# Attention and a mixture of experts on one core: the attention planned anew with other transfer times

## The chip, the core and the metric

The kernel runs on one core of a Trainium2 chip. The core has five engines with instruction queues of their own, each worked off in order: TensorE (PE in the rows; its weight loads stand apart as PEld), VectorE (DVE), ScalarE (ACT), GpSimd (POOL) and SyncE (SP), which here only issues transfers. An engine waits for another by semaphores. The metric is the device time of one execution in microseconds (us).

## What is computed

The first half is a linear attention with a complex decay, for 4 batches, 8 heads, 768 steps and a head size of 48; the second half gives its 3072 rows of 384 to 8 experts of 384 rows each and runs two matrix products per expert.

```python
mag = np.sqrt(a_re * a_re + a_im * a_im)
scale = np.minimum(mag, 0.999) / (mag + 1e-06)
a_re_n, a_im_n = (a_re * scale, a_im * scale)
...
for t in range(S):
    ar, ai = (a_re_n[:, :, t, :, None], a_im_n[:, :, t, :, None])
    new_re = ar * S_re - ai * S_im
    new_im = ar * S_im + ai * S_re
    kv = np.einsum('bhd,bhe->bhde', k[:, :, t], v[:, :, t])
    S_re, S_im = (new_re + kv, new_im)
    y[:, :, t] = np.einsum('bhd,bhde->bhe', q[:, :, t], S_re)
...
order = np.argsort(-flat)          # greedy: best score first, each expert takes N // E rows
...
h = np.maximum(x[mask] @ w1[e], 0.0)
out[mask] = h @ w2[e]
```

## The kernel before

**Tiling.** The attention is cut into 8 groups (`GROUPS`, two per batch) of three units of 128 steps: 24 units. Group 0 is worked on in two pieces (one unit, then two), group 7 too (two, then one). A group is first prepared elementwise, on tiles of 128 x 1152 (or 384 and 768 for the pieces), on ScalarE and VectorE. Each unit then has its own steps on TensorE.

**The steps and the names in the rows.** A step's short name is the key that the planner gives it; in the rows an instruction shows by the tiles that it writes and reads.

- Loads, issued by SyncE (group 0's `ai` by ScalarE): `la` is `ar<-in_a_re`, `li` is `ai<-in_a_im`, `lk` is `kq<-in_kq`, `lv` is `V<-in_v`. Of `ar` and of `ai` there is one buffer, so that the next group's load waits until the readers of this one (`F1`, `F3`, `F4` for `ar`; `F2`, `F3` for `ai`) are done.
- ScalarE, per group: `F1` (`s<-ar,cb`, a square), `F2` (`s<-ai`), `F5` (`zi<-s,cb`), `F7` (`s<-s,cb`), `F8` (`s<-zi`), `F10` (`s<-s,cb`), `G1` (`s<-zi`), `G2` (`zi<-zi`), `A1` and `A2` (`p<-p`), `T2` (`p<-neg`), and the cosine and sine, `T3` (`CS<-p,cb`) and `T1` (`CS<-neg`). Between the two sets of functions a table is loaded (ACT_TABLE_LOAD).
- VectorE, per group: `F4` (`neg<-ar`), `F3` (`p<-ar,ai`), `F6` (`s<-s,s`, the sum of `F1` and `F2`), `F9` (`zi<-s`), `F11` (`p<-p,s`), `S` (scans `zi<-zi,s`), `N0` (scans into `neg`), `N2` (`neg<-neg`), `G3` (`kq<-kq,s`) and `G5` (`kq<-kq,zi`).
- Per unit: `RQ` on VectorE multiplies by cosine and sine (`f<-kq,CS`, needs `T1` and `T3`); `K` is six transfers issued by SyncE that stack it (`KQ<-f`); on TensorE `SC` (`sc<-KQ`, scores, two halves), `FL` (`kp<-ident,KQ`), `ST` and `CA` (`U<-V,kt` and `U<-W,ident`, the carried state), `MX` (`y<-...`, the unit's output) and `FN` (`xp<-pick,xT`). VectorE masks the scores (`MK`, `am<-sc,mask`, two halves; `MX` waits for both), scales the state (`WM`, `W<-U,KQ`) and reduces the router's scores (`LR`, `lg<-xp`; after unit 17 with a maximum and a copy). ScalarE empties PSUM (`KC`, `XC`, `XE`). `BE` is five small VectorE steps on the first 18 units' scores for the router.
- `FI` are matmuls without use (`sc<-mask,f`) that keep TensorE busy ahead of a unit's scores; the table `FILL` has their number, in three portions per unit. A unit's `FI` waits for its own `RQ` and for the mask of the unit before.

**What sets the order.** The steps are put into a list with costs, wishes (`prio`, about the unit's number) and dependencies. `in_order` (line 179) then plays the engines against each other with a model of the costs: on each engine the ready step with the lowest wish plus offset (`OFF`, line 679, one number per kind of step) goes next. The order that comes out is the program's order on each engine, SyncE's transfers too; an engine never overtakes. A transfer's time in this model is made of `FLIGHT` and `ARRIVE`, and of its data time (`moved`, line 311, `K_DATA`). The model's times decide nothing else: on the chip only the order, the dependencies and `FILL` are left of it. The expert half is planned apart.

Of the kernel before, what the change touches and what calls it, by code (L numbers as in the profile page):

```python
# [21 lines left out]
B, H, S, D = 4, 8, 768, 48  # L22
N, DM, E, FF = B * S, H * D, 8, 1024
CAP = N // E
NT = N // 128
GC = 3
T = GC * 128
# [229 lines left out]
def attention(nc, real, tc, z, kq_in, a_re, a_im, v_tok, xd, later):  # L257
# [12 lines left out]
    for i in range(2):  # L270
        x = con.tile([128, GC * 384 + 16], F32, name=f"V{i}")
# [9 lines left out]
    act = nc.scalar.activation  # L281

    ops = []
    made = {}

    def op(key, eng, cost, prio, fn, deps=()):
        kind = key[0][0] if type(key[0]) is tuple else key[0]
        o = Op(eng, cost, fn, [made.get(d) for d in deps], prio)
        o.kind = kind + ("<" if prio < EARLY else ">" if prio >= LATE else "")
        ops.append(o)  # L290
        made[key] = o
        if o.kind.rstrip("<>") in ("lk", "lv"):
            moved(o, 128, (24 if key[0] == "lk" else 12) * T)
        return o

    def dve(n):
# [8 lines left out]
    def sca(n, bias=False):  # L305
        return n / 1200 + (0.19 if bias else 0.094)
# [1 line left out]
    def pool(n):  # L308
        return n / 460 + 0.08

    def moved(x, rows, nbytes):
        x.data = LOADS * rows * (9 + nbytes / 26) / 16e3

    G = len(GROUPS)
    cuts = [CUTS.get(gi, [(0, GC)]) for gi in range(G)]
# [3 lines left out]
    def get(name, gi, shape=None, p=ew, **kw):  # L319
        if (name, gi) not in tiles:  # L320
            tiles[name, gi] = p.tile(shape or [128, 3, T], F32, name=name, **kw)
        return tiles[name, gi]
# [8 lines left out]
    def last_of(stage, gi):  # L331
        return [(stage, gi, j) for j in range(len(cuts[gi]))] if gi >= 0 else []

    def free(name, stages, gi):
        return [x for s in stages for x in last_of(s, gi - BUFS[name])]
# [4 lines left out]
    def load_a(gi, j, name, src):  # L340
        b, c0, n = GROUPS[gi]
        lo, hi = cuts[gi][j]
        w = slice(lo * 384, hi * 384)
        q = nc.scalar if gi == 0 and name == "ai" else nc.sync
        return lambda: q.dma_start(
            get(name, gi, [128, 3 * T], p=ld, bufs=1)[:, w], src[b, c0 // GC, :, w])
# [17 lines left out]
    def elementwise(gi, j, at):  # L364
        b, c0, _ = GROUPS[gi]
        lo, hi = cuts[gi][j]
        n = hi - lo
# [4 lines left out]
        def G_(name, **kw):  # L372
            return get(name, gi, **kw)[..., cols]
# [4 lines left out]
        def I_(name):  # L378
            return get(name, gi)[:, lo * 384:hi * 384].rearrange("p (i t) -> p i t", i=3)

        def add(stage, eng, cost, fn, deps):
            op((stage, gi, j), eng, cost, at, fn, deps)
# [2 lines left out]
            return [(s_, gi, j) for s_ in ss]  # L385

        first = -60.0 + 30.0 * j if gi == 0 else at
        op(("li", gi, j), "dma" if gi else "act", 0.6, first - (0 if gi else 2000.0), load_a(gi, j, "ai", a_im), free("ai", ["F2", "F3"], gi))
        op(("la", gi, j), "dma", 0.6, first, load_a(gi, j, "ar", a_re), free("ar", ["F1", "F3", "F4"], gi))
        for x in ops[-2:]:  # L390
            moved(x, 128 * (1 if n == GC else 3), 12 * T if n == GC else 512 * n)
        add("F1", "act", sca(N3, True), lambda: act(G_("s1", bufs=S1_BUFS), I_("ar"), AF.Square, bias=z.cb[:, 0:1]),
            k_("la") + free("s1", ["F11", "F6"], gi))
        add("F2", *(("dve", dve(N3), lambda: v.tensor_tensor(
# [61 lines left out]
    def turns(i):  # L456
# [10 lines left out]

        f_free = [("K", i - F_BUFS), ("FI", i - F_BUFS, len(FILL.get(i - F_BUFS, ())) - 1)] if i >= F_BUFS else []
        op(("P0", i), "pool", 0.75, i, lambda: g.tensor_copy(
# [19 lines left out]
    def unit(i):  # L489
        gi, c = i // GC, i % GC  # L490
# [10 lines left out]
        def keep(n):  # L501
            if ("sc", 0) not in mine:
                mine["sc", 0] = ps.tile([128, 4, 128], F32, name="sc", bufs=2)
            for _ in range(n):
                nc.tensor.matmul(mine["sc", 0].rearrange("p h t -> p (h t)"), tiles["f", i][:, 0, 0, 128:256].bitcast(BF)[:, 1::2],
                                 z.mask.bitcast(BF)[:, None].to_broadcast([128, 2, 256]), start=True, stop=True)
        parts = FILL.get(i, ())
        for n, x in enumerate(parts):
# [100 lines left out]
        op(("FN", i), "pe", 0.9, at + 0.6, turn, [("XC", i), ("XE", i - 2), ("LR", i - 2)])  # L609
        op(("XE", i), "act", 0.371, at, out, [("FN", i), ("XS", i - 2)])  # L610
        op(("XS", i), *(("pool", 1.1) if i < NT - 2 else ("act", 0.33)), at, store, [("XE", i)])
        moved(ops[-1], 128, 4 * DM)
        op(("LR", i), "dve", 0.105 if i % 6 < 5 else 0.4, at, logits, [("FN", i)])

    def load(key, cost, at, fn, deps=()):
# [2 lines left out]
    for gi in range(G):  # L618
        for j in range(len(cuts[gi])):
            elementwise_at = gi * GC + cuts[gi][j][0]  # L620
            if j == 0:
                load(("lk", gi), 0.6, elementwise_at + 0.5, load_kq(gi), turned(gi - KQ_BUFS))
                if gi < 2:
                    load(("lv", gi), 0.6, elementwise_at + 0.6, load_v(gi))
            elementwise(gi, j, elementwise_at)
            if gi == 1:
                for x in (("lv", 0), ("lk", 1), ("lv", 1)):
                    made[x].deps.append(made["la", 1, 0])
        for c in range(GC):
            turns(gi * GC + c)  # L630
            unit(gi * GC + c)
        if gi + 2 < G:
            load(("lv", gi + 2), 0.6, elementwise_at + 4, load_v(gi + 2),
                 [("MX", gi * GC + c) for c in range(GC)] + [("ST", gi * GC + c) for c in range(GC)])
# [8 lines left out]
    for o in ops:  # L643
        o.prio += OFF.get(o.kind, 0.0)
    for o in in_order(ops, STEP, HOP, DMA_WAIT, DMA_DONE, START, SLACK):
# [25 lines left out]
BY_DMA = []  # L671
SLACK = 0.0
DMA_WAIT = 0.1
FLIGHT, ARRIVE = 1.3, 0.7
K_DATA, LOADS = 3.3, 1.15
DMA_DONE = 1.1
LATER = [2.4, 4.6, 0.9, 3.6]
START = dict(pe=0.0, act=0.3, dve=2.6, pool=4.3, dma=0.65)
OFF = {"A1": 10.399, "A2": -9.822, "BE": 0.131, "CA": -2.118, "F1": -1.107, "F10": 3.443, "F11": 7.184, "F2": -0.925, "F3": 5.421, "F4": 5.223, "F5": -4.22, "F6": 3.011, "F7": -5.852, "F8": -2.715, "F9": -5.359, "FI": 6.816, "FI<": 9.377, "FL": 9.859, "FL<": -5.873, "FN": 12.915, "G1": 1.011, "G2": -1.21, "G3": -11.062, "G4": -0.449, "G5": -6.433, "K": -5.895, "KC": -14.0, "LR": -0.075, "MK": -7.142, "MX": 7.176, "N0": 3.163, "N2": 4.716, "P0": 12.184, "RQ": 2.776, "S": 7.92, "SC": 10.153, "SC<": -1.898, "ST": 11.563, "ST<": -6.332, "T1": 8.558, "T2": 10.974, "T3": -7.584, "TL": -6.667, "WM": -3.298, "XC": -9.548, "XC<": -8.705, "XE": 10.454, "XS": 9.28, "la": -9.643, "la<": -6.574, "later": 0.869, "li": -8.149, "li<": -7.975, "lk": -3.51, "lv": -2.528, "table": -8.414}
CHAIN = ("scalar", "vector", "tensor", "gpsimd", "sync")  # L680
F_BUFS, KC_BUFS = 4, 5
FILL = {0: (6, 6, 6), 1: (2, 2, 2), 2: (4, 4, 4), 3: (2, 2, 2), 5: (6, 6, 6), 7: (4, 4, 4), 8: (1, 1, 1), 9: (3, 3, 3), 10: (1, 1, 1), 11: (3, 3, 3), 12: (3, 3, 3), 13: (2, 2, 2)}
SQ = ()
EARLY, LATE = 0, 99

# [830 lines left out]
```

## Time and profile before

| | |
|---|---|
| time, median of 3 runs | 488.61 us (488.24 to 489.17) |
| the profiled execution | 488.22 us; its span, first to last instruction, 486.4 us |
| busy in the span: PE, PEld | 430.7 us (89%), 386.3 us (79%) |
| busy in the span: DVE, ACT, POOL | 400.9 us (82%), 307.9 us (63%), 124.5 us (26%) |
| the chain that ended last | PE 69%, issue 12%, ACT 7%, DVE 6%, DMA 3% |

The attention takes the first 223 us or so of the span, the router and the experts the rest. Busy time is the time in which an engine had an instruction running; PEld lies beside PE. Matmuls are pipelined and the ends of their rows are modelled, so that the start of the next row is the better measure of how long one took. A row's idle time, in brackets, stands before the row, with what ended it.

### The profile page before, as it was taken

To read this page: it belongs to the slowest core of one execution; us is meant where nothing else is said; L and a number is where in the kernel's file an instruction comes from. 1 tells how busy PE (TensorE), PEld (TensorE's weight loads), DVE (VectorE), ACT (ScalarE), POOL (GpSimd) and SP (SyncE) were. 2 spreads that over 40 slices of the span, in tenths; PEclk is the share of its full clock that TensorE was granted. 3 is DMA by queue.
4 is the path that set the end of the run, shared out by engine and by line. 5 is a ranking of instruction groups with operands and counts; after the bars stand their busy time and mean duration, and the time that the engine had idled before them with its cause. 6 is when DMAs were issued, how large, how long until landed. Compare 5 with 4: busy or idle time off the path is not lost.

```text
span 486.4 us, 9831 instructions
## 1 busy us (share of the span) xinstructions
PE 430.7 (89%) x3632; PEld 386.3 (79%) x3632; DVE 400.9 (82%) x1023; ACT 307.9 (63%) x582; POOL 124.5 (26%) x218
## 2 busy tenths in 40 slices
PE   0019999999999999996389999999999999999996
PEld 0006887889789899985279799999999999999995
DVE  6999999999999999945869989898898999434250
ACT  7999988999889849712055538375472837442341
POOL 7321020304021411223131223140413335040202
PEclk9999999999999999998589999999999999999999
DMA  7807876868796846521162616280724438420001
GB/s 254 330 2 202 277 252 204 280 212 279 219 290 206 275 145 176 164 82 65 37 214 85 285 50 219 123 313 15 282 75 165 194 112 345 161 98 0 34 16 50
DMA packets 33104, 82.52 MB, mean 170 GB/s; under 512 B 4352, under 2 KB 23552, under 8 KB 29984
## 3 DMA queue, kind: packets, MB, share of 16 engines
q1 hardware_dynamic: 25632, 41.96, 27.6%
q0 software_dynamic: 6848, 38.95, 21.6%
q10 hardware_dynamic: 576, 0.98, 0.5%
q8 instruction: 29, 0.48, 0.4%
q14 instruction: 19, 0.16, 0.1%
HBM read 53.49 MB, written 9.44 MB: 129 GB/s over the span
## 4 chain that ended last, share of the span: by engine, by line
PE 69%; issue 12%; ACT 7%; DVE 6%; DMA 3%; POOL 1%; POOLq 1%; SPq 0%; ACTq 0%; DVEq 0%
PE acc L136 30%; PE sc L136 12%; PE y L136 8%; PE U L136 8%; PE xp L136 4%; PE kp L136 3%; ACT s L136 3%; PE cnt L136 3%; ACT p L136 1%; ACT L278 1%; DMA ai<-in_a_im 1%; DVE ind L136 1%; POOL out L136 1%; DVE neg L136 1%; DMA KQ<-f 1%
## 5 line engine op out<-in xcount | busy, mean ns | idle before, releaser
L136 PE MATMUL acc<-w2h,hh 128*128 128x384 f32 x192 | 62.5, 345 | 0.2 <-DVE hl L136 0.2
L136 PE MATMUL acc<-w2h,hl 128*128 128x384 f32 x192 | 62.1, 344 | 0.0
L136 PE MATMUL acc<-w2l,hh 128*128 128x384 f32 x192 | 61.9, 344 | 0.1
L136 PE MATMUL acc<-xl,w1h 128*128 128x384 f32 x192 | 61.2, 343 | 0.1
L136 PE MATMUL acc<-xh,w1l 128*128 128x384 f32 x192 | 61.2, 343 | 0.0
L136 PE MATMUL acc<-xh,w1h 128*128 128x384 f32 x192 | 60.0, 339 | 0.0
L136 PE MATMUL sc<-mask,f 128*128 128x512 bf16 x111 | 28.2, 400 | 35.1 <-DVE f L136 35.1
L136 ACT ACTIVATE hh<-acc 128x384 fp32r<-128x384 f32 x64 | 30.7, 491 | 38.6 <-PE acc L136 38.1
L136 POOL DMA_INDIRECT out<-ot,idx x24 | 25.5, 1063 | 105.5 <-ACT ot L136 100.4
L136 DVE SCALAR_TENSOR_TENSOR hl<-acc,hh 128x384 fp32r<-128x384 f32 x64 | 34.7, 550 | 21.6 <-ACT hh L136 21.1
L136 PEld LDWEIGHTS <-f 128*128 128x128 bf16 x111 | 10.5, 102 | 48.1 <-DVE f L136 35.1
L136 PE MATMUL sc<-KQ 96*128 96x128 f32 x384 | 48.1, 277 | 0.0
L136 PEld LDWEIGHTS sc<-KQ 96*128 96x128 f32 x384 | 45.1, 192 | 0.8 <-issue 0.7
L136 ACT ACTIVATE parts<-cnt 32x8 f32<-32x8 f32 x120 | 20.1, 168 | 39.4 <-PE cnt L136 37.2
L136 DVE TENSOR_TENSOR f<-kq,CS 128x1536 f32<-128x1536 f32 x24 | 41.6, 1749 | 1.1 <-ACT CS L136 0.7
L136 DVE TENSOR_TENSOR am<-sc,mask 128x512 f32<-128x512 f32 x48 | 31.9, 680 | 6.6 <-PE sc L136 6.2
L136 POOL DMA_DIRECT2D xd<-x x22 | 13.3, 607 | 90.6 <-ACT x L136 90.6
L136 PE MATMUL y<-am,V 128*64 128x128 f32 x384 | 36.5, 278 | 0.0
L136 PEld LDWEIGHTS acc<-w2h,hh 128*128 128x128 f32 x192 | 35.6, 189 | 0.6 <-DVE hl L136 0.6
L136 DVE TENSOR_TENSOR ind<-m,thr 128x768 bf16<-128x768 f32 (+1 forms) x45 | 33.8, 768 | 2.6 <-PE thr L136 2.3
L136 PEld LDWEIGHTS acc<-w2l,hh 128*128 128x128 f32 x192 | 35.6, 188 | 0.3 <-DVE w2l L136 0.2
L136 PEld LDWEIGHTS acc<-w2h,hl 128*128 128x128 f32 x192 | 35.7, 188 | 0.0
(203 smaller groups left out, 1109.2 us busy)
## 6 DMA issues: line engine op xcount, KB each, us to landing
KQ<-f SPq DMA_DIRECT2D x144, 128.5 KB, 2.7
kq<-in_kq SPq DMA_DIRECT2D x8, 1152.0 KB, 7.4
V<-in_v SPq DMA_DIRECT2D x8, 576.0 KB, 5.4
xd<-x POOLq DMA_DIRECT2D x22, 192.0 KB, 3.1
ar<-in_a_re SPq DMA_DIRECT2D x6, 576.0 KB, 4.5
ai<-in_a_im SPq DMA_DIRECT2D x6, 576.0 KB, 5.4
ar<-in_a_re SPq DMA_DIRECT2D x2, 384.0 KB, 5.0
ar<-in_a_re SPq DMA_DIRECT2D x2, 192.0 KB, 4.6
```

Source lines behind the costliest of these rows:

```text
L136: r = f(*a, **k)
L278: real.scalar.add_instruction(ins)
```

## The change

The planner's numbers are changed, and with them the order of the attention's steps. A transfer's data time is now a number for each kind of load, no longer worked out from its bytes; the other numbers of the transfer model, all offsets and the table of fillers are new. The steps, their tiles, buffers and dependencies stay; the fillers are 108 in place of 111, spread over the units in another way.

```diff
         if o.kind.rstrip("<>") in ("lk", "lv"):
-            moved(o, 128, (24 if key[0] == "lk" else 12) * T)
+            moved(o, RATE_Q if key[0] == "lk" else RATE_V)
...
-    def moved(x, rows, nbytes):
-        x.data = LOADS * rows * (9 + nbytes / 26) / 16e3
+    def moved(x, us):
+        x.data = us
...
-        op(("li", gi, j), "dma" if gi else "act", 0.6, first - (0 if gi else 2000.0), load_a(gi, j, "ai", a_im), free("ai", ["F2", "F3"], gi))
-        op(("la", gi, j), "dma", 0.6, first, load_a(gi, j, "ar", a_re), free("ar", ["F1", "F3", "F4"], gi))
+        op(("li", gi, j), "dma" if gi else "act", 0.43, first - (0 if gi else 2000.0), load_a(gi, j, "ai", a_im), free("ai", ["F2", "F3"], gi))
+        op(("la", gi, j), "dma", 0.43, first, load_a(gi, j, "ar", a_re), free("ar", ["F1", "F3", "F4"], gi))
         for x in ops[-2:]:
-            moved(x, 128 * (1 if n == GC else 3), 12 * T if n == GC else 512 * n)
+            moved(x, RATE_A * n / GC)
+        if not (gi or j):
+            ops[-1].data += WAKE
...
-        moved(ops[-1], 128, 4 * DM)
+        moved(ops[-1], RATE_X)
...
-FLIGHT, ARRIVE = 1.3, 0.7
-K_DATA, LOADS = 3.3, 1.15
+FLIGHT, ARRIVE = 1.38, 0.4
+K_DATA, RATE_A, RATE_Q, RATE_V, RATE_X, WAKE = 4.0, 1.3, 3.8, 1.5, 0.46, 1.0
...
-FILL = {0: (6, 6, 6), 1: (2, 2, 2), 2: (4, 4, 4), 3: (2, 2, 2), 5: (6, 6, 6), 7: (4, 4, 4), 8: (1, 1, 1), 9: (3, 3, 3), 10: (1, 1, 1), 11: (3, 3, 3), 12: (3, 3, 3), 13: (2, 2, 2)}
+FILL = {0: (6, 6, 6), 1: (4, 4, 4), 2: (2, 2, 2), 3: (3, 3, 3), 5: (1, 1, 1), 6: (6, 6, 6), 7: (2, 2, 2), 8: (3, 3, 3), 9: (1, 1, 1), 10: (4, 4, 4), 11: (1, 1, 1), 12: (1, 1, 1), 13: (1, 1, 1), 16: (1, 1, 1)}
```

`OFF`, the table of offsets, has a new number for each of its 56 kinds of step; what it does shows in the order alone. The first place is ScalarE's queue before the first cosine and sine (tiles `CS`). The tiles of 3x128 and 3x256 are group 0's two pieces; 1152 wide are groups 1 and 2. Before:

```order
L136 ACTIVATE zi<-zi 128x3x256
L136 ACTIVATE s_310<-ar,cb 128x1152
L136 ACTIVATE s_270<-s_270,cb 128x1152
L278 ACT_TABLE_LOAD
L136 ACTIVATE s_323<-ai 128x1152
L136 ACTIVATE CS<-neg 128x3x128
L136 ACTIVATE CS<-neg 128x3x256
L136 ACTIVATE p<-neg 128x3x128
L136 ACTIVATE CS<-p,cb 128x3x128
L136 ACTIVATE p<-neg 128x3x256
L136 ACTIVATE CS<-p,cb 128x3x256
```

The same place in the changed kernel:

```order
L136 ACTIVATE p<-neg 128x3x128
L136 ACTIVATE s_135<-zi 128x3x256
L136 ACTIVATE zi<-zi 128x3x256
L136 ACTIVATE s_297<-ar,cb 128x1152
L136 ACTIVATE zi<-s_297,cb 128x1152
L136 ACTIVATE p<-neg 128x3x256
L136 ACTIVATE s_297<-zi 128x1152
L136 ACTIVATE s_312<-ai 128x1152
L136 ACTIVATE s_251<-s_251,cb 128x1152
L136 ACTIVATE s_316<-ar,cb 128x1152
L136 ACTIVATE s_251<-s_251,cb 128x1152
L278 ACT_TABLE_LOAD
```

Both `T2` of group 0 (`p<-neg`) and group 2's `F2` (`s_323<-ai` before, `s_312<-ai` now) have moved ahead of group 2's `F1` (`s_310<-ar,cb` before, `s_316<-ar,cb` now). After the table load the four `CS` follow, `T1` of the first piece as the third of them.

The second place is VectorE's queue just before the first `RQ` (`f_117<-kq,CS`). Before, from group 1's nine scans on:

```order
L136 SCALAR_TENSOR_TENSOR zi<-zi,s_270 128x128 x9
L136 TENSOR_TENSOR s_323<-s_323,s_310 128x1152
L136 TENSOR_TENSOR f_117<-kq,CS 128x6x256
L136 TENSOR_TENSOR f_118<-kq,CS 128x6x256
L136 TENSOR_TENSOR f_119<-kq,CS 128x6x256
```

In the changed kernel:

```order
L136 TENSOR_TENSOR s_312<-s_312,s_316 128x1152
L136 SCALAR_TENSOR_TENSOR zi<-zi,s_251 128x128 x9
L136 SCALAR_TENSOR_TENSOR p<-ar,ai 128x1152
L136 TENSOR_TENSOR f_117<-kq,CS 128x6x256
L136 TENSOR_SCALAR neg<-ar 128x1152
L136 TENSOR_TENSOR f_118<-kq,CS 128x6x256
L136 TENSOR_TENSOR f_119<-kq,CS 128x6x256
```

Group 2's `F6` (the sum `s_312<-s_312,s_316`) now stands ahead of group 1's scans, and group 2's `F3` (`p<-ar,ai`) has come in ahead of the first `RQ`.

The third place is VectorE's queue at unit 19's two masks, with the tiles' numbers. Before they are `am_2080` and `am_2094`:

```order
L136 TENSOR_TENSOR am_2080<-sc_2062,mask_65 128x512
L136 TENSOR_SCALAR neg_1837<-neg_1837 128x3x256
L136 TENSOR_TENSOR am_2094<-sc_2072,mask_65 128x512
L136 TENSOR_TENSOR kq_1786<-kq_1786,zi_1702 128x6x128
```

Now they are `am_2096` and `am_2104`:

```order
L136 TENSOR_REDUCE lg2_89<-xp_2032 128x16
L136 TENSOR_REDUCE ext_93<-lg2_89 128x2
L136 COPY lg2_89<-ext_93 128x16
L136 TENSOR_REDUCE top_90<-lg2_89 128x18
...
L136 TENSOR_TENSOR oh_92<-q18_2058,qm_91 128x144
L136 TENSOR_SCALAR neg_1625<-neg_1625 128x3x256
L136 TENSOR_TENSOR W1_111<-U_2063,KQ3_124 96x384
L136 TENSOR_TENSOR kq_1782<-kq_1782,zi_1690 128x6x128
L136 TENSOR_TENSOR am_2096<-sc_2075,mask_65 128x512
L136 TENSOR_TENSOR am_2104<-sc_2084,mask_65 128x512
```

`LR` of unit 17 with its maximum and copy, the five steps of `BE` (from `top_90` to `oh_92`) and `G5` of group 7's first piece (`kq_1782<-kq_1782,zi_1690`) stood behind these masks and stand ahead of them now.

## Rows read from the trace of the kernel before

**Rows 1.** One stretch: us, busy us (x rows) of PE, PEld, DVE, ACT, POOL; clock, DMA.

```profile
35.10:190.00 154.90, 154.62 (x1537) 130.20 (x1538) 153.16 (x221) 136.34 (x169) 29.52 (x43) 1.00 0.76 233
```

**Rows 2.** Waits (us, times, longest): TensorE's, 36 to 222.9; VectorE's longest, 36 to 208.

```profile
PE kp L136 <- DMA KQ<-f: 0.2, 1, 0.2
...
DVE am L136 <- PE sc L136: 0.8, 3, 0.4
```

**Rows 3.** Timeline of ScalarE, 12 to 35 us: start, us, operation, tiles.

```profile
12.92 0.92 ACT L136 ACTIVATE s<-s,cb 128x768 f32<-128x768 f32 x1
...
26.18 1.24 ACT L136 ACTIVATE s<-ar,cb 128x1152 f32<-128x1152 f32 x1
...
29.88 1.16 ACT L136 ACTIVATE s<-ai 128x1152 f32<-128x1152 f32 x1
...
32.09 0.51 ACT L136 ACTIVATE p<-neg 128x384 f32<-128x384 int32 x1
...
33.16 0.83 ACT L136 ACTIVATE p<-neg 128x768 f32<-128x768 int32 x1
34.01 0.94 ACT L136 ACTIVATE CS<-p,cb 128x768 f32<-128x768 f32 x1
```

**Rows 4.** Timeline of VectorE up to the first `RQ`.

```profile
6.60 0.95 DVE L136 SCALAR_TENSOR_TENSOR p<-ar,ai 128x768 f32<-128x768 f32 x1
...
15.08 1.36 DVE L136 SCALAR_TENSOR_TENSOR p<-ar,ai 128x1152 f32<-128x1152 f32 x1
...
28.60 2.95 DVE L136 TENSOR_TENSOR_SCAN zi<-zi,s 128x128 f32<-128x128 f32 x9
31.46 1.33 DVE L136 TENSOR_TENSOR s<-s,s 128x1152 f32<-128x1152 f32 x1
33.28 5.20 DVE L136 TENSOR_TENSOR f<-kq,CS 128x1536 f32<-128x1536 f32 x3 [0.49 <-ACT CS L136]
```

**Rows 5.** Timeline of TensorE: its start, an `FN`, a run of fillers.

```profile
35.10 5.95 PE L136 MATMUL sc<-mask,f 128*128 128x512 bf16 x18 [35.10 <-DVE f L136]
...
100.45 1.07 PE L136 MATMUL xp<-pick,xT 112*128 112x112 f32 x8
101.36 1.96 PE L136 MATMUL sc<-KQ 96*128 96x128 f32 x16
...
107.18 2.12 PE L136 MATMUL sc<-mask,f 128*128 128x512 bf16 x9
```

**Rows 6.** Timelines at unit 19: TensorE's `ST` and `MX`, then VectorE.

```profile
189.19 1.48 PE L136 MATMUL U<-V,kt 128*96 128x48 f32 x16
...
191.29 0.44 PE L136 MATMUL y<-am,V 128*64 128x128 f32 x4
...
190.18 0.67 DVE L136 TENSOR_TENSOR am<-sc,mask 128x512 f32<-128x512 f32 x1
190.77 0.94 DVE L136 TENSOR_TENSOR kq<-kq,zi 128x768 f32<-128x768 f32 x1
191.64 0.55 DVE L136 TENSOR_TENSOR p<-p,s 128x384 f32<-128x384 f32 x1
...
200.12 0.22 DVE L136 TENSOR_REDUCE lg<-xp 128x16 f32<-128x64 f32 x1
...
202.53 0.22 DVE L136 TENSOR_REDUCE lg<-xp 128x16 f32<-128x64 f32 x1
```

**Rows 7.** Transfers by kind: queue, count, KB each, median us to landing.

```profile
KQ<-f SPq DMA_DIRECT2D x144, 128.5 KB, 2.7
...
ai<-in_a_im SPq DMA_DIRECT2D x6, 576.0 KB, 5.4
```

**Rows 8.** Timelines near the attention's end: VectorE, then TensorE.

```profile
206.07 1.76 DVE L136 TENSOR_TENSOR f<-kq,CS 128x1536 f32<-128x1536 f32 x1 [0.19 <-ACT CS L136]
207.74 0.55 DVE L136 TENSOR_TENSOR W<-U,KQ 96x384 f32<-96x384 f32 x1
...
215.54 2.05 PE L136 MATMUL sc<-KQ 96*128 96x128 f32 x16
```

More of the change, by code (lines that the diff above doesn't have):

```diff
@@ L678 @@
 START = dict(pe=0.0, act=0.3, dve=2.6, pool=4.3, dma=0.65)
-OFF = {"A1": 10.399, "A2": -9.822, "BE": 0.131, "CA": -2.118, "F1": -1.107, "F10": 3.443, "F11": 7.184, "F2": -0.925, "F3": 5.421, "F4": 5.223, "F5": -4.22, "F6": 3.011, "F7": -5.852, "F8": -2.715, "F9": -5.359, "FI": 6.816, "FI<": 9.377, "FL": 9.859, "FL<": -5.873, "FN": 12.915, "G1": 1.011, "G2": -1.21, "G3": -11.062, "G4": -0.449, "G5": -6.433, "K": -5.895, "KC": -14.0, "LR": -0.075, "MK": -7.142, "MX": 7.176, "N0": 3.163, "N2": 4.716, "P0": 12.184, "RQ": 2.776, "S": 7.92, "SC": 10.153, "SC<": -1.898, "ST": 11.563, "ST<": -6.332, "T1": 8.558, "T2": 10.974, "T3": -7.584, "TL": -6.667, "WM": -3.298, "XC": -9.548, "XC<": -8.705, "XE": 10.454, "XS": 9.28, "la": -9.643, "la<": -6.574, "later": 0.869, "li": -8.149, "li<": -7.975, "lk": -3.51, "lv": -2.528, "table": -8.414}
+OFF = {"A1": 9.751, "A2": -1.604, "BE": -9.451, "CA": -3.175, "F1": 14.0, "F10": 10.208, "F11": 7.986, "F2": 9.812, "F3": 4.206, "F4": -3.946, "F5": -11.121, "F6": 5.232, "F7": 14.0, "F8": -3.512, "F9": -13.732, "FI": -1.801, "FI<": -8.456, "FL": 7.245, "FL<": 6.06, "FN": 7.748, "G1": 7.746, "G2": 4.998, "G3": 0.778, "G4": -7.467, "G5": 9.958, "K": 5.06, "KC": -0.115, "LR": 5.57, "MK": -4.977, "MX": -5.019, "N0": 8.339, "N2": 7.333, "P0": -4.932, "RQ": 1.118, "S": 8.085, "SC": 6.632, "SC<": 0.356, "ST": 1.846, "ST<": 10.725, "T1": -2.371, "T2": 3.331, "T3": -7.062, "TL": -5.281, "WM": -9.815, "XC": -1.802, "XC<": -6.059, "XE": 12.999, "XS": 14.0, "la": 1.112, "la<": 6.817, "later": -6.31, "li": 8.502, "li<": -1.935, "lk": 9.862, "lv": 1.51, "table": -5.45}
 CHAIN = ("scalar", "vector", "tensor", "gpsimd", "sync")
 F_BUFS, KC_BUFS = 4, 5
-FILL = {0: (6, 6, 6), 1: (2, 2, 2), 2: (4, 4, 4), 3: (2, 2, 2), 5: (6, 6, 6), 7: (4, 4, 4), 8: (1, 1, 1), 9: (3, 3, 3), 10: (1, 1, 1), 11: (3, 3, 3), 12: (3, 3, 3), 13: (2, 2, 2)}
+FILL = {0: (6, 6, 6), 1: (4, 4, 4), 2: (2, 2, 2), 3: (3, 3, 3), 5: (1, 1, 1), 6: (6, 6, 6), 7: (2, 2, 2), 8: (3, 3, 3), 9: (1, 1, 1), 10: (4, 4, 4), 11: (1, 1, 1), 12: (1, 1, 1), 13: (1, 1, 1), 16: (1, 1, 1)}
 SQ = ()
```

## The prediction

> **What bounds the kernel now.** I read the table of stretches first. From 35.1 to 190 us, 154.90 us, TensorE is busy for 154.62 at a granted clock of 1.00, which is 2.4 GHz, and VectorE for 153.16 [rows 1]. Two full queues leave it open which of them makes the time, so I read the waits next. TensorE's list for 36 to 222.9 us has one entry, 0.2 us; VectorE's longest is 0.8 us, and that is for TensorE's scores [rows 2]. So TensorE's queue, fillers included, runs from its first filler at 35.10 [rows 5] to the last `FN` without a hole. The attention ends at the start of that queue, plus its work, plus what waits come into it. The timelines then give each piece. Behind the attention the router and the experts stand in the same order as before.
>
> That the queue's end and not the last transfer decides is seen near the end. The last `RQ` ends at 206.07 + 1.76 = 207.83, and its unit's scores begin at 215.54 [rows 8]. One of the six transfers between takes 2.7 us from issue to landing [rows 7]; they would fill the 7.7 us only if issuing the six took 5.
>
> **The change, part by part.** *Start of TensorE.* The first filler waits for the first `RQ`, and this waits for what VectorE and ScalarE have ahead of it. Before, ScalarE's `F1` of group 2 ran from 26.18 to 27.42 [rows 3]. Now three more steps stand ahead of it and none fewer: `T2` of the first piece, 0.51; `T2` of the second, 33.16 to 34.01, 0.85; `F2` of group 2, 1.16, less the 0.08 by which a row there reaches over the start of the next, 1.08 [rows 3]. ScalarE's rows follow each other without idle time, so `F1` ends at 27.42 + 0.51 + 0.85 + 1.08 = 29.86. On VectorE group 2's `F6` needs it, and now the scans of group 1, group 2's `F3` and the `RQ` are queued behind `F6`: 1.33 - 0.08 = 1.25, then 31.46 - 28.60 = 2.86, then 1.36 - 0.08 = 1.28 [rows 4]. The first `RQ` starts at 29.86 + 1.25 + 2.86 + 1.28 = 35.25 in place of 33.28: 1.97 us later. Its other condition, `T1` of the first piece, comes earlier than that: all six of `T1`, `T2`, `T3` were through at 34.01 + 0.94 = 34.95 [rows 3], and what ScalarE has ahead of the `T1` now is not more than that. TensorE begins 1.97 us later and, with its queue full, ends 1.97 us later.
>
> *Fillers.* Three fewer, nine of them taking 2.12 us [rows 5]: 0.24 each at most, 0.7 us saved. Where the others stand within the queue moves nothing as long as the queue is full. The cover that they were for, a wait for VectorE or for the `K` transfers, is priced next.
>
> *A new wait at unit 19.* `MX` of a unit waits for its two masks, and everything on TensorE is queued behind it. Before, the second mask of unit 19 ended at 190.18 + 0.67 = 190.85 and `MX` began at 191.29 [rows 6], 0.44 us later. Now VectorE has more ahead of that mask: `LR` of unit 17 and `BE`, 202.53 - 200.12 = 2.41 us, and `G5` of group 7's first piece, 191.64 - 190.77 = 0.87 us [rows 6]. To this comes its later start, of which group 2's `F3`, done ahead of the `RQ` now, gives 1.28 back: 1.97 - 1.28 = 0.69. The mask ends at 190.85 + 2.41 + 0.87 + 0.69 = 194.82. TensorE has less ahead of this `MX`: `ST` and `CA` of unit 19 have gone behind it, 191.29 - 189.19 = 2.10 [rows 6], three fillers are gone, 0.7, and `FN` of units 17 and 18 have come in, 101.36 - 100.45 = 0.91 each [rows 5]. It would reach `MX` at 191.29 + 1.97 - 2.10 - 0.7 + 1.82 = 192.28. So it waits 2.54 us in all up to there, wherever in the queue the wait falls. That supposes VectorE keeps every wait that it had. The 0.8 us for scores [rows 2] should go, since VectorE now comes to its masks later against TensorE: 1.74. The bounds are 2.54 and, if VectorE gains elsewhere what the row does not show, nothing. I take 1.7, because the only waits in VectorE's list that the new order can remove for sure are those for scores. Behind `MX` the rest of TensorE's queue has to run, so that nothing is given back.
>
> *Masks and state behind the last `RQ`.* Unit 20's `WM` and unit 21's two masks have moved behind the last `RQ`: 0.55 - 0.08 for the one [rows 8], 0.67 - 0.08 for each of the others [rows 6], 1.65 us in all. The last `RQ` then ends at 207.83 + 0.69 - 1.65 = 206.87. This costs or saves nothing while TensorE's queue is what the scores of unit 23 wait for. What stalls next if TensorE waited less is this chain.
>
> *The loads* change places on SyncE; I set them at nothing, as each is still issued ahead of its group's `K` transfers. The one without cover is priced as a rival.
>
> **The sum.** 1.97 - 0.7 + 1.7 = 3.0 us. On the profiled execution's 488.22 us that is 491.2; this execution lies 0.39 below the median of the runs, 488.61, and the forecast for the median is **491.6 us**. With the wait's two ends it goes from 489.9 to 492.4.
>
> **A rule weighed.** Rows 1 call TensorE full, and rows 2 say that it hardly waits. The Trainium skill, page "Perfetto Trace Analysis", section "Identifying the Most-Contended Engine", holds that matmul busy time is no measure for TensorE, as matmuls are pipelined; one should judge by the weight loads' busy share and take the engine of highest occupancy. By that rule TensorE would have room here, 130.20 / 154.90 = 84%, and VectorE would be the bound at 153.16 / 154.90 = 99%, so that the result would be the third rival's below. The trace agrees on VectorE's share, but a share of weight loads is not a wait, and the list of waits shows none that could be shortened: I go by the rows.
>
> **Rivals.** *Only the later start counts.* VectorE makes up its 2.5 us before unit 19 and the wait does not come: 488.61 + 1.97 - 0.7 = 489.9. For it: VectorE's dense rows leave no proof of how each would run beside other neighbours. Against it: VectorE's listed waits for scores are 0.8 us, a third of what it would have to make up. 15 in 100.
>
> *A load comes late.* Group 1's `F2` now stands ahead of the row at 12.92 [rows 3], and its `ai` can be issued only when `F3` of group 0 is through, 6.60 + 0.95 = 7.55 [rows 4]. With 5.4 us to landing [rows 7] it lands at 12.95, with no margin. Each microsecond later moves `F1` of group 2, the first `RQ` and all of TensorE's queue by one: 1 to 2 us more give 492.6 to 493.6. 12 in 100.
>
> *VectorE's queue makes the time.* If TensorE could take its late start and its waits out of slack that the rows don't show, the end would follow the last `RQ`: 206.87 against 207.83, 1.0 us earlier, and 1.8 if the 0.8 us of waits vanish as well. That is 487.6 to 486.8 us. It decides from the point where TensorE has 3 us in hand. For it: VectorE's 99%. Against it: TensorE's scores of the last unit began 7.7 us behind the last `RQ`, and its queue was shown full. 7 in 100.
>
> *Nothing that can be measured.* The orders differ, but the late start is made up by waits of ScalarE or transfers in the first 30 us that I overrate. 6 in 100.
>
> **How the numbers follow.** The forecast has 60 in 100, the other cases 15, 12, 7 and 6. From no change a time can be told here by about 0.2%, 1.0 us. Slower by more than that, above 489.6, are the forecast, the first rival but for its lowest part, and the second: 0.85. Within 0.2%: 0.08. Faster: 0.07. The range takes in the first rival and the second, from 489.6 to 493.6; the forecast's own is 490.4 to 492.6.
>
> **What would show it.** In the changed kernel's trace the first filler starts at about 37.1 on TensorE, and VectorE waits for ScalarE's `s` ahead of its `F6` at 30 us. TensorE's list of waits has 1 to 3 us more for VectorE's `am` or what VectorE has ahead of it, up to unit 20. `FN` of the last unit starts about 3 us later, and the stretch behind it is as long as before. The forecast is wrong if the first filler starts before 36 us, or if TensorE still waits for nothing.

## The result, and the profile after

The changed kernel takes 491.4 us (median of 5 runs, 490.84 to 492.49) against 488.61: the ratio is 1.0051, 95% interval 1.0034 to 1.0068. It is slower, by 1.7 to 3.3 us. The profiled execution took 491.04 us, its span 489.3, against 488.22 and 486.4.

Where the time went is read from two places. The first is the end of the attention, the row of the last two `FN`. In the timeline of TensorE, in the kernel before:

```profile
221.20 2.04 PE L136 MATMUL xp<-pick,xT 112*128 112x112 f32 x16
```

and in the changed kernel, its start, the steps behind it, and its end:

```profile
37.07 6.82 PE L136 MATMUL sc<-mask,f 128*128 128x512 bf16 x18 [37.07 <-DVE f L136]
43.73 1.95 PE L136 MATMUL sc<-KQ 96*128 96x128 f32 x16
45.51 0.82 PE L136 MATMUL kp<-ident,KQ 96*128 96x96 f32 x8
46.34 1.02 PE L136 MATMUL sc<-mask,f 128*128 128x512 bf16 x4
...
223.84 2.04 PE L136 MATMUL xp<-pick,xT 112*128 112x112 f32 x16
```

The attention ends 2.64 us later. Of the 2.8 us between the two profiled executions, only 0.2 lie behind it: the stretch from there to the end of the span is 263.40 us long against 263.16. The table of stretches, before and then changed:

```profile
223.24:486.40 263.16, 242.88 (x1730) 226.23 (x1728) 196.56 (x703) 122.47 (x345) 69.34 (x73) 0.96 0.36 134
...
225.90:489.30 263.40, 243.07 (x1729) 226.29 (x1728) 196.60 (x703) 122.39 (x345) 69.21 (x73) 0.96 0.36 134
```

The second place is the start. TensorE begins at 37.07 in place of 35.10 [rows 5], 1.97 us later, because the first `RQ` does. Timeline of VectorE in the changed kernel, up to it:

```profile
28.68 0.76 DVE L136 TENSOR_SCALAR zi<-s 128x1152 f32<-128x1152 f32 x1 [0.84 <-ACT s L136]
29.88 1.36 DVE L136 TENSOR_TENSOR s<-s,s 128x1152 f32<-128x1152 f32 x1 [0.44 <-ACT s L136]
31.16 2.94 DVE L136 TENSOR_TENSOR_SCAN zi<-zi,s 128x128 f32<-128x128 f32 x9
34.01 1.33 DVE L136 SCALAR_TENSOR_TENSOR p<-ar,ai 128x1152 f32<-128x1152 f32 x1
35.26 1.75 DVE L136 TENSOR_TENSOR f<-kq,CS 128x1536 f32<-128x1536 f32 x1
```

VectorE waits for ScalarE's square of group 2 and then has `F6`, the scans and `F3` ahead of the `RQ`, each as long as before [rows 4]. ScalarE has that square (`s<-ar,cb`) at 28.55, where it was at 26.18 [rows 3], and group 1's `F2` at 12.81 waits for nothing:

```profile
12.81 1.15 ACT L136 ACTIVATE s<-ai 128x1152 f32<-128x1152 f32 x1
...
28.55 1.24 ACT L136 ACTIVATE s<-ar,cb 128x1152 f32<-128x1152 f32 x1
```

The list of TensorE's waits from 37.2 to 225 us has again one entry of 0.2 us [rows 2]:

```profile
PE sc L136 <- DVE am L136: 0.2, 1, 0.2
```

From TensorE's first filler to the last two `FN` the stretch is 0.67 us longer, and its idle time, the stretch less the busy time, went from 0.28 to 0.41. The table of stretches, before and then changed:

```profile
35.10:221.20 186.10, 185.82 (x1887) 158.15 (x1887) 174.14 (x260) 152.90 (x197) 37.06 (x56) 1.00 0.70 214
...
37.07:223.84 186.77, 186.36 (x1885) 159.36 (x1885) 171.51 (x259) 151.73 (x196) 42.57 (x56) 1.00 0.69 213
```

At unit 19, where the prediction has a wait of 1.7 us, TensorE's timeline shows:

```profile
192.66 1.07 PE L136 MATMUL xp<-pick,xT 112*128 112x112 f32 x8
193.66 0.44 PE L136 MATMUL y<-am,V 128*64 128x128 f32 x4
```

VectorE's has the unit's two masks in one row:

```profile
192.53 1.28 DVE L136 TENSOR_TENSOR am<-sc,mask 128x512 f32<-128x512 f32 x2
```

The second mask ends at 192.53 + 1.28 = 193.81, and `MX` begins at 193.66, right behind an `FN` and before that end. So the first mask is all that its start needs, and the line on `MX` in the first part, by which it waits for both, is too strict for its first matmul.

One thing more differs: the fillers ahead of unit 0. The table of stretches over those at the slower pace (the count stands behind TensorE's busy time), in the kernel before:

```profile
35.10:38.90 3.80, 3.80 (x9) 1.00 0.49 131
```

and in the changed kernel:

```profile
37.07:42.60 5.53, 5.53 (x14) 1.95 (x15) 5.53 (x5) 5.49 (x6) 0.85 (x2) 1.00 0.78 242
```

Nine fillers in 3.80 us, 0.42 each, and 14 starts in 5.53, the last of them already fast; the rest take 0.22, half as much, as at the higher clock. (The clock's column says 1.00 here all the same; it does not show the pace of these rows.) The row behind the 18 starts at 43.73 now (above), and in the kernel before at 40.92:

```profile
40.92 0.85 PE L136 MATMUL kp<-ident,KQ 96*128 96x96 f32 x8
```

So the 18 together took 35.10 to 40.92 before and 37.07 to 43.73 now, 6.66 against 5.82: 0.84 us more.

### The profile page after: what moved, and what is told of

It is laid out like the page before. It is cut to its first block, busy times and chain, and to the rows that moved or that the text cites. A ratio compares the mean times of both kernels' runs of the same rounds, so it can differ in the third digit from the quotient of the medians.

```text
span 489.3 us, 9834 instructions
## 1 busy us (share of the span) xinstructions
PE 431.5 (88%) x3629; PEld 387.5 (79%) x3629; DVE 399.0 (82%) x1023; ACT 308.6 (63%) x582; POOL 126.9 (26%) x218
## 4 chain that ended last, share of the span: by engine, by line
PE 62%; issue 12%; DVE 11%; ACT 6%; DMA 5%; POOL 1%; SPq 1%; POOLq 1%; ACTq 0%; DVEq 0%
PE acc L136 30%; PE sc L136 10%; PE y L136 7%; PE U L136 6%; PE xp L136 3%; PE cnt L136 3%; ACT s L136 2%; PE kp L136 2%; DVE f L136 2%; DVE zi L136 2%; DMA KQ<-f 2%; SPq L136 1%; DMA ar<-in_a_re 1%; DMA ai<-in_a_im 1%; DVE ind L136 1%
## 5 line engine op out<-in xcount | busy, mean ns | idle before, releaser
L136 PE MATMUL sc<-mask,f 128*128 128x512 bf16 x108 | 29.3, 410 | 37.4 <-DVE f L136 37.1
L136 PEld LDWEIGHTS sc<-KQ 96*128 96x128 f32 x384 | 46.1, 192 | 3.8 <-issue 1.6
L136 PEld LDWEIGHTS acc<-xh,w1l 128*128 128x128 f32 x192 | 35.7, 188 | 0.0
```

Source lines behind the costliest of these rows:

```text
L136: r = f(*a, **k)
```

## The experiments

All were timed in five rounds beside the kernel before. An effect of 1 us is smaller than most of these intervals can tell, so the end of the attention in the trace of one execution is given beside each ratio. Steps are named as in the first part. "Moved" means that the planner's order is frozen and then that step alone is put elsewhere in it.

| run | first filler | last two `FN` start | against 221.20 | ratio to before |
|---|---|---|---|---|
| changed kernel | 37.07 | 223.84 | +2.64 | 1.0051 [1.0034, 1.0068] |
| RQ of unit 0 twice (on before) | 36.82 | 223.04 | +1.84 | 1.0024 [0.9999, 1.0049] |
| nine fillers more (on before) | 35.08 | 224.00 | +2.80 | 1.0024 [1.0000, 1.0047] |
| 36 fillers fewer (on before) | 35.15 | 224.48 | +3.28 | 1.0056 [1.0034, 1.0078] |
| F3 of group 5 twice (on before) | 34.92 | 221.75 | +0.55 | 1.0011 [0.9999, 1.0023] |
| 27 fillers fewer (on changed) | 37.01 | 224.23 | +3.03 | 1.0069 [1.0046, 1.0092] |
| 15 fillers at unit 0 (on changed) | 37.03 | 223.44 | +2.24 | 1.0040 [1.0017, 1.0064] |
| BE behind unit 22's first mask (on changed) | 36.92 | 223.26 | +2.06 | 1.0040 [1.0014, 1.0066] |
| BE behind the last RQ (on changed) | 36.95 | 226.71 | +5.51 | 1.0106 [1.0079, 1.0134] |
| head of before (on changed) | 35.08 | 224.39 | +3.19 | 1.0073 [1.0049, 1.0096] |
| F3 of group 2 behind the RQs (on changed) | 36.79 | 232.42 | +11.22 | 1.0229 [1.0204, 1.0255] |
| changed up to unit 18, then before | 36.84 | 223.61 | +2.41 | 1.0053 [1.0034, 1.0071] |
| before up to unit 18, then changed | 35.09 | 227.13 | +5.93 | 1.0128 [1.0104, 1.0151] |

Two such ends differ by chance too. Unit 2's scores start at 57.6 us in the kernel before. In three runs of its order whose edit lies behind that point they start 0.24 earlier (`F3` of group 5 twice), 0.23 later (nine fillers more) and 0.89 later (36 fewer). The two later ones wait longer for `KQ` than the 0.20 of the kernel before. TensorE's timelines, nine fillers more and then 36 fewer:

```profile
50.56 0.85 PE L136 MATMUL kp<-ident,KQ 96*128 96x96 f32 x8 [0.45 <-DMA KQ<-f]
...
51.23 0.85 PE L136 MATMUL kp<-ident,KQ 96*128 96x96 f32 x8 [1.04 <-DMA KQ<-f]
```

So a difference of less than about 1 us between two ends says little by itself; where in the trace the lag arises says more.

**A late start of both queues.** In the kernel before, the first `RQ` is done twice.

```diff
-        op(("RQ", i), "dve", dve(1536), i, rot, X("T1", "T3", "G3", "G5") + f_free)
+        op(("RQ", i), "dve", dve(1536), i, lambda: [rot() for _ in range(1 + (i == 0))], X("T1", "T3", "G3", "G5") + f_free)
```

> The kernel before, with the RQ of unit 0 done twice on VectorE (the same values, 1.76 us more), so that the first filler and the first transfers start 1.76 later and nothing else is changed. My prediction's step on the start (a first RQ that is late by so much moves the end by as much): 1.76 us slower, ratio 1.0036. Rival (the late start is taken out of slack that the fillers hide): under 0.5 us, ratio 1.001 or less.

The ratio, 1.0024, lies between the two and tells neither apart. In the trace TensorE starts 1.72 us later and the attention ends 1.84 later:

```profile
36.82 5.53 PE L136 MATMUL sc<-mask,f 128*128 128x512 bf16 x18 [36.82 <-DVE f L136]
...
223.04 2.04 PE L136 MATMUL xp<-pick,xT 112*128 112x112 f32 x16
```

In the order of before, a first `RQ` that is late so moves the end by about as much. That the two numbers lie so near is in part chance: unit 2's scores start only 1.28 later, and a wait of 0.45 at 111 us brings the lag to 1.92. And the second `RQ` holds back VectorE as well: unit 0's first mask starts at 46.16 in place of 44.68. The run tells what a late start of both queues costs, not one of TensorE alone.

**TensorE with more or with less to do.** Nine fillers more at unit 10 of the kernel before; then 36 fewer (units 9 to 13) of the kernel before; then 27 fewer (units 9 to 13 and 16) of the changed kernel.

```diff
-            op(("FI", i, n), "pe", 0.213 * x, at - 0.4, lambda x=x: keep(x), [("RQ", i), ("MK", i - 1, 0), ("SC", i - 1, 1), ("FI", i, n - 1)])
+            op(("FI", i, n), "pe", 0.213 * x, at - 0.4, lambda x=x: keep(x + 3 * (i == 10)), [("RQ", i), ("MK", i - 1, 0), ("SC", i - 1, 1), ("FI", i, n - 1)])
```

The other two, the planned order as it was (the table is that of the first of them):

```diff
-            op(("FI", i, n), "pe", 0.213 * x, at - 0.4, lambda x=x: keep(x), [("RQ", i), ("MK", i - 1, 0), ("SC", i - 1, 1), ("FI", i, n - 1)])
+            op(("FI", i, n), "pe", 0.213 * x, at - 0.4, lambda x=EMIT.get(i, FILL[i])[n]: keep(x), [("RQ", i), ("MK", i - 1, 0), ("SC", i - 1, 1), ("FI", i, n - 1)])
...
+EMIT = {i: (0, 0, 0) for i in (9, 10, 11, 12, 13)}
```

> The kernel before, with nine more fillers at unit 10, 1.95 us more of TensorE, VectorE's queue unchanged. If TensorE's queue sets the end (what my prediction rests on): 1.95 us slower, ratio 1.0040. If VectorE sets the pace there and TensorE only waits less: no change. Coupled queues (a mask on VectorE follows its scores by 0.04 us at many units, so that a delay of either engine reaches the other, while relief of one alone turns into a wait): 1 to 1.95 slower, and RQ of unit 12 comes later by as much.

> The kernel before, without its 36 fillers of units 9 to 13, which take 36 x 0.216 = 7.8 us of TensorE. Theory Q, on which my prediction rests (TensorE's queue, fillers included, has no hole and sets the end): 7.8 us faster. Theory V (up to the first RQ of the last full group, unit 18, VectorE's queue sets the pace and TensorE has slack that its fillers hide; from there on TensorE's queue runs dense): no change within 0.5 us, RQ of unit 18 still starts at about 173 us, and in the fillers' place stand waits of TensorE of a microsecond each.

> The changed kernel without the 27 fillers of units 9 to 13 and 16, which take 27 x 0.216 = 5.8 us of TensorE. Theory Q in its pure form (TensorE's queue is the only bound): 491.4 - 5.8 = 485.6. Theory V (masks and scans come when VectorE has them, and TensorE would wait in the fillers' place): 491.4 less 0.5 at most, and the list of TensorE's waits shows some 5 us more for VectorE's am and f. Between the two: the difference tells how much slack VectorE has against TensorE.

More work costs in full in the trace: the attention ends 2.80 us later for 1.95 us of fillers. Of this 0.23 was there ahead of the added fillers (the wait of 0.5 below, shown above at 50.56), 1.94 came with them and 0.63 with a new wait of 0.7 at 189.5. The ratio alone allows anything from nothing to 2.3 us. Waits with nine fillers more:

```profile
PE kp L136 <- PE y L136: 0.7, 1, 0.7
PE kp L136 <- DMA KQ<-f: 0.5, 1, 0.5
```

Less work brings nothing. Without 27 fillers the changed kernel's attention ends 0.39 us later than with them, and in their place stand 5.6 us of idle time, nearly all of it waits for VectorE, ScalarE and the transfers:

```profile
PE y L136 <- DVE W L136: 2.4, 3, 1.1
PE xp L136 <- ACT xT L136: 0.9, 1, 0.9
PE y L136 <- issue: 0.8, 1, 0.8
PE y L136 <- ACT zi L136: 0.6, 1, 0.6
PE U L136 <- ACT kt L136: 0.6, 1, 0.6
PE sc L136 <- DMA KQ<-f: 0.3, 1, 0.3
```

Without 36 the kernel before waits likewise, 7.6 us for 7.8 us of fillers, the most of it here:

```profile
PE kp L136 <- DMA KQ<-f: 3.9, 3, 2.0
PE y L136 <- ACT xT L136: 1.6, 2, 1.2
PE kp L136 <- ACT s L136: 1.3, 1, 1.3
```

It ends 3.28 us later all the same. Of this 0.89 was there at unit 2, ahead of the first filler taken out. For the rest, with one of these waits, 2.01 us up to 110.15, a stretch of 6.83 us begins at a granted clock of 0.50, which is 1.2 GHz, and half of it is lost:

```profile
109.96:116.79 6.83, 6.64 (x40) 6.45 (x42) 5.53 (x11) 4.35 (x8) 1.08 (x2) 0.50 0.84 239
```

So pure Q, by which every filler counts, is wrong for relief, and pure V, by which TensorE has slack, is wrong for delay. The coupled reading of the first of the three texts fits best. The fillers stand where TensorE would otherwise wait; a queue without holes that contains them doesn't show that this queue alone makes the time.

**VectorE with more to do.** In the kernel before, `F3` of group 5 is done twice, 1.4 us more right ahead of the `RQ` of unit 12.

```diff
-        add("F3", "dve", dve(N3), lambda: v.scalar_tensor_tensor(
-            G_("p", bufs=2), I_("ar"), TINY, I_("ai"), op0=OP.add, op1=OP.mult), k_("la", "li") + free("p", ["T3"], gi))
+        add("F3", "dve", dve(N3), lambda: [v.scalar_tensor_tensor(
+            G_("p", bufs=2), I_("ar"), TINY, I_("ai"), op0=OP.add, op1=OP.mult) for _ in range(2 if gi == 5 else 1)], k_("la", "li") + free("p", ["T3"], gi))
```

> The kernel before, with F3 of group 5 done twice on VectorE (the same product written twice, 1.3 us more at about 100 us); nothing else changes. Theory V: the time goes up by the whole of it, 1.3 us, and RQ of unit 18 starts 1.3 later. Theory Q: TensorE has masks in hand by 1 to 9 us in that stretch, so no change.

The end comes 0.55 us later. TensorE lags by 0.05 just ahead of the doubled step, and its list then shows a wait of 0.5, `PE y` for ScalarE's `xT`, where it had none. So about a third of what was added reached TensorE, and VectorE had some 0.9 us of slack against it there. V was too high by 0.8 and Q too low by 0.5.

**The wait at unit 19.** The changed kernel with the router's maximum and copy put into `BE`, and `BE` moved out of the masks' way, first behind the last `RQ`, then behind the first mask of unit 22.

```diff
-            if i == NT - 7:
-                v.tensor_reduce(z.ext, z.lg2[:, :i + 1].rearrange("p c a e -> p a c e"), op=OP.max, axis=AX.XY)
-                v.tensor_copy(z.lg2[:, NT], bc(z.ext, E))
...
+        v.tensor_reduce(z.ext, z.lg2[:, r].rearrange("p c a e -> p a c e"), op=OP.max, axis=AX.XY)
+        v.tensor_copy(z.lg2[:, NT], bc(z.ext, E))
...
+MOVES = [(('BE', 0), ('RQ', 23))]
```

In the second run the step named last is `('MK', 22, 0)`.

> The changed kernel, with the maximum and the copy for the router's logits put into BE, and BE moved from between the masks of units 17 to 19 to behind the last RQ: some 2.2 us of VectorE leave the place ahead of the masks of units 19 to 23. My prediction's wait at unit 19 (1.7 us) would go: 489.7. Theory Q as the trace of the changed kernel has it (the waits there are only some 0.5 us in all): at most 0.5 saved, 490.9 to 491.4. Theory V: the last RQ comes 2.2 us earlier, and the end with it: 489.2.

> The changed kernel, with the maximum and the copy for the router's logits put into BE, and BE moved into the stretch of 3.4 us behind the first mask of unit 22 in which VectorE is idle there. My prediction's wait at unit 19 (1.7 us, of which these steps are 2.41 us of VectorE) goes with it: 1.7 faster than the changed kernel, about 1.0016 of before. From the trace of the changed kernel, in which TensorE waits for 0.5 us in all and hardly at unit 19: no more than 0.3 faster, about 1.0045 of before.

The first place was a bad one: `BE` there delays the masks of unit 21, and TensorE waits 1.39 us for them, and then runs 3.41 us at half the clock. TensorE's timeline:

```profile
208.82 1.48 PE L136 MATMUL sc<-KQ 96*128 96x128 f32 x8 [1.39 <-DVE am L136]
```

The stretch at half the clock, with the clock in the third column from the end:

```profile
209.51:212.92 3.41, 3.41 (x31) 3.19 (x31) 0.69 (x1) 0.00 (x0) 0.00 (x0) 0.50 0.30 77
```

In the second place it fits into VectorE's idle time. The attention ends 0.58 us before that of the changed kernel, but 0.5 of it were there at the `RQ` of unit 18 already (174.5 against 175.0), ahead of anything that was moved. 2.2 us less on VectorE ahead of the masks of units 19 to 22 gain 0.1 at most: no wait of 1.7 us was there to take away.

**Fillers of unit 0.** The changed kernel with 15 in place of 18.

```diff
+EMIT = {0: (5, 5, 5)}
```

> The changed kernel, with 15 in place of the 18 fillers of unit 0, of which 13 ran at half the clock there and 9 before. If the longer fillers cost what they took (0.84 us more than before): three fewer save 0.65, SC of unit 0 starts that much earlier, about 1.0038 of before. If the transfers of unit 0 land no earlier than the fillers end: no change, about 1.0051, and TensorE waits for KQ instead.

The ratio can't tell the two cases apart. In the trace the 15 end at 43.07, 0.66 before the 18 did, but the next fillers, those of unit 1, start at 46.29, nearly where they did (46.34), since they wait for the mask of unit 0:

```profile
43.07 2.01 PE L136 MATMUL sc<-KQ 96*128 96x128 f32 x16
44.92 0.82 PE L136 MATMUL kp<-ident,KQ 96*128 96x96 f32 x8
46.29 1.02 PE L136 MATMUL sc<-mask,f 128*128 128x512 bf16 x4 [0.55 <-DVE am L136]
```

So neither the three fillers nor the slower pace of some of them counts for more than 0.1 us here. With all 18, but only nine of them slow, the run with `BE` behind unit 22's mask waited there as well:

```profile
46.19 1.02 PE L136 MATMUL sc<-mask,f 128*128 128x512 bf16 x4 [0.66 <-DVE am L136]
```

Of the 0.40 by which the attention's end comes earlier, 0.33 arises at 61 us: there the changed kernel pauses between two matmuls of an `MX`, ahead of `y<-KQ,W`, and this run does not, nor do two of the other runs of this order.

**The start undone in the changed kernel.** First the whole head (`HEAD` names 96 steps), then `F3` of group 2 alone.

```diff
+    done = in_order(ops, STEP, HOP, DMA_WAIT, DMA_DONE, START, SLACK)
+    head = [made[k] for k in HEAD]
+    for o in head + [o for o in done if o not in head]:
```

```diff
+MOVES = [(('F3', 2, 0), ('RQ', 2))]
```

> The changed kernel, with its first 96 steps (all engines, up to the third first RQ) in the order of the kernel before and the rest in the changed order. Theory Q (TensorE's queue sets the end: its start, its work, its half-speed fillers and its waits): the first RQ starts at about 33.3 us in place of 35.26 and the first filler at 35.1 in place of 37.07; if the clock also rises after 9 in place of 13 half-speed fillers, 0.84 more is saved; 491.4 - 1.97 - 0.84 = 488.6, and 489.4 without the clock's part. Theory V (VectorE's queue of masks and scans sets the end, and TensorE's late start is taken out of slack): VectorE gets only the 1.28 of group 2's F3 and less back before the first RQ but has it to do behind it, so under 0.7 is saved: 490.7 or more.

> The changed kernel, with one step moved: F3 of group 2 (1.28 us on VectorE) from ahead of the first RQ to behind the third. Theory Q: TensorE starts 1.28 earlier, at 35.8, and ends as much earlier: 490.1, or up to 0.8 less if fewer fillers run at half speed. Theory V: VectorE's work is the same up to unit 1's masks, so no change: 491.4 within 0.3.

The first went against Q and fits V (490.7 or more), the second fits neither. With the old head TensorE starts at 35.08, but then has to wait 2.12 us for the first mask of unit 0. VectorE, with `F3` of group 2 still to do and no idle time from its first `RQ` to that mask, brings it only 0.62 us earlier. VectorE's timeline, with the old head and then in the changed kernel:

```profile
44.98 1.27 DVE L136 TENSOR_TENSOR am<-sc,mask 128x512 f32<-128x512 f32 x2
...
45.60 1.28 DVE L136 TENSOR_TENSOR am<-sc,mask 128x512 f32<-128x512 f32 x2
```

Half the clock for 3.42 us follows the wait, and the gain is lost again. So in the changed order an earlier start of TensorE turns into a wait for that mask: the late start and this wait stand in for each other. TensorE's timeline:

```profile
42.77 0.82 PE L136 MATMUL kp<-ident,KQ 96*128 96x96 f32 x8
45.71 1.86 PE L136 MATMUL sc<-mask,f 128*128 128x512 bf16 x4 [2.12 <-DVE am L136]
```

and the stretch behind the wait:

```profile
45.65:49.07 3.42, 3.36 (x20) 1.98 (x19) 3.42 (x5) 1.98 (x2) 0.59 (x1) 0.50 0.99 235
```

With `F3` moved, SyncE is what stops: group 3's `ai` needs the buffer that `F3` reads and stands ahead of all `K` transfers on SyncE, which are issued from 42.46 in place of 37.09. SyncE's timeline:

```profile
42.08 0.33 SPq L136 DMA_DIRECT2D ai<-in_a_im  x1
42.46 11.72 SPq L136 DMA_DIRECT2D KQ<-f  x18
```

TensorE waits for them:

```profile
50.21 2.05 PE L136 MATMUL sc<-KQ 96*128 96x128 f32 x8 [7.34 <-DMA KQ<-f]
```

In the new order `F3` of group 2 has to stand ahead of the first `RQ`, for that load's sake. The experiment is no test of the start.

**Two halves.** One order up to the `RQ` of unit 18, the other behind it; the orders are written out as lists of steps.

```diff
-    for o in in_order(ops, STEP, HOP, DMA_WAIT, DMA_DONE, START, SLACK):
-        o.fn()
+    for k in ORDER:
+        made[k].fn()
```

> Order of the changed kernel (with its fillers) up to the RQ of unit 18, order of the kernel before behind it. Theory V: RQ of unit 18 at 175.0 and its scores at 184.2 as in the changed kernel, then the dense stretch of before: 1.9 us slower than before. My prediction's steps: the later start less the fillers, 1.97 - 0.7 = 1.3 slower than before, without the wait at unit 19. The two agree within 0.6; it is run with the other half to see whether the two parts add up to the whole, 2.7.

> Order of the kernel before (with its fillers) up to the RQ of unit 18, order of the changed kernel behind it. Theory V: RQ of unit 18 at 173.1 as before, its scores 9.2 us later, and then the changed order's dense stretch of TensorE, which was 0.8 us longer from those scores to the last FN: 0.8 us slower than before, and 1.9 faster than the changed kernel. My prediction's steps: without the late start, but with the wait at unit 19: 1.7 or more slower than before.

With the changed order only up to unit 18 the attention ends 2.41 us late, nearly all of the 2.64: the loss lies ahead of unit 18, and the order behind it costs nothing that could be seen. The other half is no test. At the seam ScalarE has a table load and three elementwise steps of group 7 ahead of the `xT` that an `FN` needs. TensorE waits for it:

```profile
181.88 2.05 PE L136 MATMUL xp<-pick,xT 112*128 112x112 f32 x8 [2.77 <-ACT xT L136]
```

and half the clock comes with the wait:

```profile
180.88:187.70 6.82, 5.82 (x41) 5.29 (x42) 5.40 (x14) 4.19 (x9) 1.47 (x4) 0.50 0.58 170
```

No run points to an order that beats the kernel before.

## Why the prediction was right, and where not

The forecast, 491.6 us, and the measured 491.4 agree, and the sign was right. That the number came so near is luck: of the three terms of the sum two were wrong, and they were made up for by what the prediction did not price. One of its own signs of being wrong, that TensorE still waits for nothing, came true (one wait of 0.2).

- **Start of TensorE, +1.97: the size right, the path not shown.** The first `RQ` was put at 35.25 and came at 35.26, through the steps that the prediction names: ScalarE's `F1` of group 2 ended at 28.55 + 1.24 = 29.79 (29.86 was said), and VectorE's `F6`, scans and `F3` stood between. That the end moves because TensorE's queue is full is another matter. The doubled `RQ` moved it by about as much, but held back VectorE too; and with the old head TensorE started on time and lost 2.12 us to the wait for unit 0's mask.
- **Three fewer fillers, -0.7: too large.** The step took every filler for work of a full queue. Counted from the start of each row to the next, the fillers behind the first 18 took 20.15 us in place of 20.37, 0.2 less. Taking away 27 or 36 gained nothing, and taking away three at unit 0 at most 0.1 at that place.
- **The wait at unit 19, +1.7: this step failed.** It put the second mask's end at 194.82, which came at 193.81, and TensorE at `MX` at 192.28, while it got there at 193.66. So even with both masks needed the wait would have been 0.15. It also took `MX` to need both when it starts, which the rows of the changed kernel contradict. Moving 2.2 us out of VectorE's way there gained 0.1 at most, and with the order of before from unit 18 on the loss is 2.41 all the same.
- **State and masks behind the last `RQ`, loads: nothing, right.** The last `RQ` ended at 204.69 + 1.76 = 206.45 (206.87 was said), and the end did not follow it. The load with no margin was in time, so the second rival did not come. VectorE's timeline in the changed kernel:

```profile
204.69 1.76 DVE L136 TENSOR_TENSOR f<-kq,CS 128x1536 f32<-128x1536 f32 x1 [1.25 <-ACT CS L136]
```

The two wrong terms together were +1.0; in their place the trace has 2.64 - 1.97 = 0.67. Counted from the start of each row to the next, TensorE's first 18 fillers took 0.84 more, the other fillers 0.22 less, the rest of its rows 0.07 less, and idle time grew by 0.13, which is that difference within rounding.

This sum does not yet say what caused it. The 18 fillers end 2.81 late and the attention 2.64 late, and the order behind unit 18 costs nothing that could be seen: the loss is there within the first microseconds of TensorE's queue. There the fillers of unit 1 start at 46.1 to 46.3 us in the changed kernel and in three runs of its order that came to that point earlier (15 fillers, `BE` behind unit 22's mask, changed up to unit 18) and waited 0.5 to 0.7 for VectorE's mask of unit 0. So VectorE's late start holds this place as much as TensorE's does. That some 2 us come from the first `RQ` being late, through both queues, fits the doubled `RQ`; it is not shown in the changed order, in which no run has both the old start and that mask early. Those three runs ended 2.1 to 2.4 late, 0.2 to 0.7 more than they started; why the changed kernel pauses at 61 us and they do not stays open. The first rival, *only the later start counts*, was nearer to the mechanism, as it had no wait at unit 19, but it too subtracted the fillers.

The third rival, by which the end follows the last `RQ`, is refuted: the last `RQ` came 1.4 us earlier and the end 2.64 later. What the prediction took from the Trainium skill ("Perfetto Trace Analysis", section "Identifying the Most-Contended Engine"), that VectorE would be the bound, is not borne out as a rule for the whole: 2.2 us taken off it ahead of units 19 to 22 gained 0.1 at most. But the reading against it, that a full queue of TensorE leaves only TensorE, was too simple: in these runs 1.95 us more on TensorE cost all of it, 1.4 us more on VectorE cost 0.5, relief of either alone brought nothing, and at unit 0 VectorE's queue set the time.

## What to carry to other kernels

Fillers hide waits: where matmuls without use stand in a queue, a list of waits without entries doesn't say that the engine is the bound; ask what each filler waits for and what would be late in its place. In two queues that feed each other unit by unit, count a delay of both ahead of the first unit in full, and count an earlier start of one engine, or work taken off it, at nothing until the trace shows the other engine ready earlier. Before a wait is predicted from a step with several inputs, look at which of them its first instruction reads.

## What the runs showed of the hardware

Longer idle times of TensorE cost more than themselves. Waits of 1.39, 2.01, 2.12, 2.77 and 7.34 us were each accompanied by 3.4 or 6.8 us at a granted clock of 0.50 (1.2 GHz), from within the wait or at most 0.7 us behind it; waits of 0.5 to 1.3 us in the runs with fewer fillers were not.

Of the fillers at the start of TensorE a different number ran at the slower pace in each execution: in fourteen traces, 7 to 14 of them took over 0.3 us to the next one. With the head of before and one first `RQ` it was 9, 9, 8, 11, 9 and 14. At 0.21 us each that is up to 1.3 us under the same order of steps.

Issuing takes SyncE's time: 18 `K` transfers took 11.7 us in a row, 0.65 each, in the kernel before, in the changed one and with `F3` moved alike, so that one load ahead of them that can't be issued yet holds up all of them.
